# A fused attention and mixture kernel: a copy moved from VectorE to GpSimd, small factors written with gaps, other fillers and another order

## The chip, the cores and the metric

The kernel runs on one core of one Trainium2 chip. The metric is the device time of one execution in microseconds, the median of several runs. A core has five engines that work side by side: PE (TensorE, matrix products), DVE (VectorE), ACT (ScalarE), POOL (GpSimd) and SP (SyncE, which here only issues transfers). Each works through its own instructions in the order in which they were written.

## What is computed

Three stages, each feeding the next: attention over 4 x 8 heads with 576 positions of 64 numbers, a soft mixture of 8 experts with 4 slots each, and a gated layer. All inputs are 32-bit floats in memory (the last layer's weights come in 64 bits and are converted on the chip).

```
# attention: mask is 32 back, plainly, or 128 back at every fourth place
scores = scale * q @ k.T ; scores = where(mask, scores, -1e9)
attn = exp(scores - max(scores)) ; attn = attn / (sum(attn) + 1e-9)
x = (attn @ v) laid out as 2304 x 512
# soft mixture
logits = x @ phi
d = softmax of logits over the tokens ; slot_input = d.T @ x
slot_out[e] = relu(slot_input[e] @ w1[e]) @ w2[e]
c = softmax of logits over the slots ; x = c @ slot_out
# gated layer
h = x @ w_in ; out = (h * sigmoid(h)) @ w_out
```

## The kernel before

Attention is worked through in sixteen pairs of heads, n = 0 to 15; a pair has its 576 positions in nine blocks of 64 (the constant NJ), and only blocks near the diagonal are formed. For each pair the steps are these, by the names that the order uses:

- `lq`, `lk`, `lv`: loads of q, k and v, issued on SP. All three have a few regions only, which pairs take in turn (two for q and v, three for k), so a load waits until an earlier pair has used its region up.
- `qx`, `qy`: q is copied out to a spread form with zeros in the gaps, one half of the partitions each (`spread`, L158 on POOL and L156 on DVE); the region `qreg` is `ra_a` for even pairs, `rb_a` for odd ones, and a copy into it also waits for the scores of the pair two earlier.
- `vx`, `vy`: v masked to two halves (`vmask`): two copies on POOL (L175), and one multiplication on DVE (L179) or ACT (L177) in turn.
- `M`, `S`: the mask and then the scores into PSUM, on PE (`masks`, `scores`; in the profile the scores are the group of 36 records with `rk_k` and `ra_a` or `rb_a`).
- `rm`: maximum of each row and block (L207), then the nine maxima times minus the scale (L208), both on DVE.
- `ex`: nine exponentials on ACT (L212), each with its sum.
- `rc`: the nine sums plus 1e-9 (L224) and their reciprocals (L225), on DVE.
- `nm`: the block times its reciprocals, on POOL (L228).
- `pt`: four transposes on DVE (L235 to L241).
- `pv`: the product with v on PE (`pv0.0` and `pv0.1` are the first pair's), `xe` its copy out on ACT, `T` the transposes of it on PE (L279), `lt` its share of the logits on PE (`ltmm`: four products over the first 512 positions and four over the last 128; the name `lb` is their PSUM bank), `te` the copy of `T` on ACT.

All matrix products are written through one helper, `mm`, on L81. Behind attention come the first expert products (`L1`, sixteen 1 MB weights `w1`), the second (`L2`, weights `w2`), then the gated layer. The loads of the weights are issued on the same queue as q, k and v. In which order is set by a string, ATT, of which each letter is one load in turn: w a weight, v one of v, q one of q and its k.

The order of everything else comes from `list_schedule`: each operation has an engine, a cost and the operations it depends on, and the function goes through a simulated time in which each engine takes the ready operation with the longest way to the end, plus an addition by kind from the table PRIO. Its result is the order of the instructions on each engine; at run time an engine waits at an instruction until what it depends on is done. The loads q, k, v and w are bound to ATT's order. The fillers (`fl0`, `fl1`, `fl2`) are products of a constant tile `cc` whose result nobody reads; the table FILL says how many go ahead of the scores of pair 0, and of the masks of pairs 1 and 2.

## Time and profile before

| | us |
|---|---|
| median of 3 runs | 374.77 |
| the three runs | 371.95, 374.77, 374.87 |
| the profiled execution | 374.85 |
| its span in the trace | 373.1 |
| PE busy | 348.3 (93%) |
| DVE busy | 250.2 (67%) |
| ACT busy | 166.2 (45%) |
| POOL busy | 66.8 (18%) |

The shares are means over three stages that are unlike: attention (to 88 us, with a tail to 108), the mixture, and the gated layer. POOL works in the first and in part of the second only. The rows are therefore read by stretches of time, and instructions by the line that wrote them. A timeline's row is the start, the length, the engine, the line, the operation, what it writes and reads; in brackets the idle time ahead of it and what ended that. In a group's row the sum and the mean length stand after the first bar, the idle time before the group and its releasers after the second.

### The profile page before, as it was taken

Reading aid. Unit: us, or ns where it says so; the run is one execution under the profiler, and the core shown is the slowest. Engines: PE = TensorE matmul, PEld = TensorE weight load, DVE = VectorE, ACT = ScalarE, POOL = GpSimd, SP = SyncE. Lnnn points to the kernel's source line nnn. Section 1 sums busy time; section 2 is a strip of 40 time slices with the busy share of each in tenths; the row PEclk is TensorE's granted clock in tenths of the full one; section 3 lists DMA queues with packets and bytes.
Section 4 is the critical chain, followed back from the end, with each engine's and each line's share of the span. In section 5 each row is a group of like instructions: output and inputs, shape, how many; then the busy total and the mean of one; then the engine's idle time right before and its main releaser. Section 6 shows DMA issues by size and latency. Waiting matters only on the chain.

```text
span 373.1 us, 8272 instructions
## 1 busy us (share of the span) xinstructions
PE 348.3 (93%) x3269; PEld 268.8 (72%) x3269; DVE 250.2 (67%) x552; ACT 166.2 (45%) x558; POOL 66.8 (18%) x105
## 2 busy tenths in 40 slices
PE   7698788888989999999999999999999999999995
PEld 3587677676743337778888888878788888888883
DVE  6878998788641069999999974368443654474335
ACT  2768778867521036668434242265542222222210
POOL 6566646754341020000000000000000000000000
PEclk9879999999999999999999999999999999999998
DMA  8999999999599999663433000000000310031004
GB/s 264 366 328 399 332 408 406 389 376 399 198 422 387 419 408 422 276 227 112 181 158 112 2 0 0 3 0 2 1 0 2 112 56 2 0 113 58 0 0 170
DMA packets 17462, 70.04 MB, mean 188 GB/s; under 512 B 1936, under 2 KB 2448, under 8 KB 11664
## 3 DMA queue, kind: packets, MB, share of 16 engines
q1 hardware_dynamic: 17424, 69.53, 48.4%
q8 instruction: 25, 0.41, 0.4%
q14 instruction: 13, 0.11, 0.1%
HBM read 64.80 MB, written 4.72 MB: 186 GB/s over the span
## 4 chain that ended last, share of the span: by engine, by line
PE 76%; DVE 10%; ACT 5%; DMA 5%; issue 2%; POOL 1%; SPq 0%; DVEq 0%; ACTq 0%; POOLq 0%
PE ps L81 74%; DMA rs_raw<-in_q 5%; DVE stats L207 2%; ACT rt_px L212 2%; PE ps L279 1%; PE ps L389 1%; DVE stats L208 1%; DVE ra_a L241 1%; POOL rt_px L228 1%; DVE rb_a L156 1%; ACT rv_astk L659 1%; ACT rt_px L268 1%; DVE ra_a L239 1%; DVE ra_a L237 0%; DVE x_gz L752 0%
## 5 line engine op out<-in xcount | busy, mean ns | idle before, releaser
L81 PE MATMUL ps<-w_ws,x_gz 128*128 128x512 f32 x432 | 109.4, 392 | 0.0
L742 ACT ACTIVATE rt_gtm<-ps 128x384 f32<-128x384 f32 x96 | 46.9, 491 | 102.4 <-PE ps L81 102.3
L81 PEld LDWEIGHTS ps<-w_ws,x_gz 128*128 128x128 f32 x432 | 80.2, 188 | 16.5 <-DVE w_ost L834 0.3
L81 PE MATMUL ps<-w_ws,w_gy 128*128 128x512 f32 (+1 forms) x219 | 55.9, 390 | 0.3 <-DVE w_gy L749 0.3
L212 ACT ACTIVATE rt_px<-ps,stats 128x64 f32<-128x64 f32 x144 | 43.4, 331 | 17.4 <-DVE stats L208 7.5
L81 PEld LDWEIGHTS ps<-w_ws,w_gy 128*128 128x128 f32 x219 | 40.2, 188 | 9.2 <-DVE w_gy L749 0.7
L749 DVE CAST x_gz<-rt_gtm 128x384 fp32r<-128x384 f32 x52 | 18.6, 357 | 39.3 <-ACT rt_gtm L742 39.1
L752 DVE TENSOR_TENSOR x_gz<-rt_gtm,x_gz 128x384 fp32r<-128x384 f32 x64 | 35.6, 557 | 4.3 <-DVE x_gz L749 0.5
L81 PE MATMUL ps<-ct_ct,rv_astk 128*128 128x384 f32 x96 | 32.6, 341 | 0.6 <-DVE lg L637 0.4
L212 ACT ACTIVATION_READ_ACCUMULATOR rt_px<-ps,stats 128x1 f32 x144 | 32.0, 222 | 0.0
L175 POOL COPY rv_v<-rs_raw 32x576 f32<-32x576 f32 x32 | 21.1, 658 | 15.3 <-PE ps L81 10.2
L81 PE MATMUL ps<-ra_a,rv_v 128*64 128x96 f32 (+2 forms) x320 | 16.8, 255 | 6.5 <-DVE ra_a L241 5.8
L81 PEld LDWEIGHTS ps<-ct_ct,rv_astk 128*128 128x128 f32 x96 | 17.9, 187 | 6.5 <-DVE lg L637 1.2
L749 DVE CAST w_gy<-rt_gtm 128x384 fp32r<-128x384 f32 x28 | 10.0, 357 | 18.7 <-ACT rt_gtm L742 18.6
L81 PEld LDWEIGHTS ps<-ra_a,rv_v 128*64 128x64 f32 x320 | 15.1, 148 | 8.5 <-DVE ra_a L241 3.2
L228 POOL TENSOR_TENSOR rt_px<-rt_px,stats 128x576 f32<-128x576 f32 x16 | 18.9, 1184 | 9.9 <-DVE stats L225 5.2
L752 DVE TENSOR_TENSOR w_gy<-rt_gtm,w_gy 128x384 fp32r<-128x384 f32 x32 | 17.9, 558 | 2.8 <-ACT rt_gtm L742 0.8
L81 PE MATMUL ps<-rk_ws,x_gz 128*128 128x512 f32 x72 | 18.7, 395 | 0.7 <-ACT x_gz L747 0.7
L81 PE MATMUL ps<-rb_ws,x_gz 128*128 128x512 f32 x72 | 18.4, 393 | 0.0
L279 PE MATMUL ps<-ip,rt_px 128*128 128x128 f32 x80 | 12.5, 288 | 3.8 <-ACT rt_px L268 2.3
L81 PEld LDWEIGHTS ps<-rk_ws,x_gz 128*128 128x128 f32 x72 | 13.2, 188 | 3.8 <-ACT x_gz L747 1.1
L81 PE MATMUL ps<-rb_a,rv_v 128*64 128x96 f32 (+2 forms) x320 | 15.0, 240 | 0.7 <-DVE rb_a L241 0.7
(210 smaller groups left out, 519.2 us busy)
## 6 DMA issues: line engine op xcount, KB each, us to landing
w_wi<-in_w_in SPq DMA_DIRECT2D x7, 1024.0 KB, 10.3
w_wo<-in_w_out SPq DMA_DIRECT2D x5, 1024.0 KB, 6.9
rs_raw<-in_q SPq DMA_DIRECT2D x16, 288.0 KB, 7.3
rk_k<-in_k SPq DMA_DIRECT2D x16, 288.0 KB, 7.5
rs_raw<-in_v SPq DMA_DIRECT2D x16, 288.0 KB, 7.1
out<-w_ost SPq DMA_DIRECT2D x17, 256.0 KB, 2.1
rs_wo<-in_w_out SPq DMA_DIRECT2D x2, 1024.0 KB, 9.3
ct_w1.0_201<-in_w SPq DMA_DIRECT2D x1, 1024.0 KB, 7.0
```

The lines of the kernel that those rows point to most:

```text
L81: pe.matmul(out, lhsT=lhsT, rhs=rhs, start=start, stop=stop, skip_group_check=True)
L156: dve.tensor_scalar(out=out, in0=src, scalar1=1.0, scalar2=None, op0=ALU.mult)
L175: pool.tensor_copy(out[r, :, z, :], raw[r])
L207: dve.tensor_reduce(out=mxs[:, n % 2], in_=ps[:, c:c + 64 * NJ].rearrange("p (j c) -> p j c", c=64), axis=AXX, op=ALU.max)
L208: dve.tensor_scalar(out=nmx[:, n % 2], in0=mxs[:, n % 2], scalar1=-(D ** -0.5), scalar2=None, op0=ALU.mult)
L212: act.activation(out=preg(n)[:, j, :], in_=sj(n, j), func=ACTF.Exp, scale=D ** -0.5, bias=nmx[:, r, j:j + 1], accum_out=sums[:, r, j:j + 1])
L228: pool.tensor_tensor(out=preg(n), in0=preg(n), in1=rinv[:, n % 2].rearrange("p (j o) -> p j o", o=1).to_broadcast([128, NJ, 64]), op=ALU.mult)
L239: dve.transpose(out=t[64:128, :, 32:64], in_=p[64:128, :, 32:64])
L279: pe.transpose(ps[:, c:c + 128], x[:, tok(t):tok(t) + 128], ident)
L742: act.activation(out=gtm(u), in_=hb(u), func=ACTF.Silu)
L749: dve.tensor_copy(ghalf(u, 0), gtm(u))
L752: dve.tensor_tensor(out=ghalf(u, 1), in0=gtm(u), in1=ghalf(u, 0), op=ALU.subtract)
```

## The change

Five things change.

1. For pairs 1 to 15 the second half of q, `qy`, is copied by POOL as the first half is (QP lists the pairs). Pair 0 keeps DVE.
2. The nine negated maxima (`nmx`) and the nine sums plus 1e-9 (now `sume`) move from `stats` to a tile `spaced`, in which three numbers are followed by a gap of one. They are read from nine numbers in a row and written as three by three. The reciprocals are read from the gaps' form and written in a row.
3. FILL: seven instead of nine fillers ahead of the first scores, and a new group of nine, `fl3`, ahead of the first value product `pv0.0` (behind the scores of pair 2). The constant tile that fillers read is set over 256 columns, not 640.
4. The last four products of `ltmm` become two, g = 2 and 3: positions 448 to 511, which the first four have too, are no longer formed twice. The half of the bank that is not written any more is set once to -1e30 (`ilb`).
5. The costs that the scheduler goes by, the table PRIO (89 kinds of operation, 87 of them with another number) and ATT are new.

```diff
@@ tiles
-    stats = cp.tile([128, 4, 2, NJ], F32, name="stats")
-    mxs, nmx, sums, rinv = (stats[:, i] for i in range(4))
+    stats = cp.tile([128, 3, 2, NJ], F32, name="stats")
+    spaced = cp.tile([128, 2, 2, 3, 4], F32, name="spaced")
+    mxs, sums, rinv = (stats[:, i] for i in range(3))
+    nmx, sume = (spaced[:, i, :, :, 0:3] for i in range(2))
@@ spread
-        if z:
+        if z and n not in QP:
             dve.tensor_scalar(out=out, in0=src, scalar1=1.0, scalar2=None, op0=ALU.mult)
         else:
             pool.tensor_copy(out, src)
@@ rowmax, exps, recip
-        dve.tensor_scalar(out=nmx[:, n % 2], in0=mxs[:, n % 2], scalar1=-(D ** -0.5), scalar2=None, op0=ALU.mult)
+        dve.tensor_scalar(out=nmx[:, n % 2], in0=mxs[:, n % 2].rearrange("p (a b) -> p a b", b=3), scalar1=-(D ** -0.5), scalar2=None, op0=ALU.mult)
...
-                       bias=nmx[:, r, j:j + 1], accum_out=sums[:, r, j:j + 1])
+                       bias=nmx[:, r, j // 3, j % 3:j % 3 + 1], accum_out=sums[:, r, j:j + 1])
...
-        dve.tensor_scalar(out=rinv[:, r], in0=sums[:, r], scalar1=EPS, scalar2=None, op0=ALU.add)
-        dve.reciprocal(out=rinv[:, r], in_=rinv[:, r])
+        dve.tensor_scalar(out=sume[:, r], in0=sums[:, r].rearrange("p (a b) -> p a b", b=3), scalar1=EPS, scalar2=None, op0=ALU.add)
+        dve.reciprocal(out=rinv[:, r].rearrange("p (a b) -> p a b", b=3), in_=sume[:, r])
@@ ltmm
-        for g in range(4):
+        for g in range(2, 4):
             mm(lb[32 * g:32 * g + 32, 128:160], phi, x[:, 448 + 32 * g:480 + 32 * g], False, p == 3)
@@ operations of a pair
-            op(f"q{'xy'[z]}{n}", ("POOL", "DVE")[z], (.72, .68)[z], [...], lambda n=n, z=z: spread(n, z))
+            op(f"q{'xy'[z]}{n}", "DVE" if z and n not in QP else "POOL", .66, [...], lambda n=n, z=z: spread(n, z))
...
-            op(f"pv{n}.{k}", "PE", (1.41, .25)[k], [f"vx{n}", f"vy{n}"] + ...
+            op(f"pv{n}.{k}", "PE", (1.41, .25)[k], ["fl3" if not n else None] + [f"vx{n}", f"vy{n}"] + ...
@@ fillers and first values
+    op("ilb", "DVE", .1, [], lambda: dve.memset(lb[0:64, 128:160], -1e30))
-    op("ifl", "DVE", .6, [], lambda: dve.memset(cc, 1.0))
+    op("ifl", "DVE", .3, [], lambda: dve.memset(cc.rearrange("p t r s -> p (t r s)")[:, 0:256], 1.0))
@@ tables
-ATT = "wvwqwqvqvqwqvwqqvwvwqwvwqvqwvwvqwqwvvqwwvwwwvw"
+ATT = "wvqwwqvqvwqvwqwqvwqvvqqvwqwwvwvqwqvvwqvwwvwwww"
-FILL = {0: 9, 1: 6, 2: 6}
+FILL = {0: 7, 1: 6, 2: 6, 3: 9}
+QP = range(1, 16)
```

What the order becomes at three places follows. In it L228 of before is L230 of after, L175 is L177, L158 is L160, L207 and L208 are L209 and L210, L224 and L225 are L226 and L227, and the lines of the transposes are two higher.

On POOL, around the normalisation of pair 8. L158 (L160) is a copy of q into the region of an even (`ra_a0`) or odd (`rb_a1`) pair, L175 (L177) the two mask copies of a v, L228 (L230) a normalisation; `x2` is two instructions in a row. Before, from the copy for pair 10 to the copy for pair 12:

```order
L158 COPY ra_a0_107<-rs_raw_111 64x18x32
L228 TENSOR_TENSOR rt_px_112<-rt_px_112,stats_77 128x576
L175 COPY rv_v_110<-rs_raw_111 32x9x64 x2
L228 TENSOR_TENSOR rt_px_112<-rt_px_112,stats_77 128x576
L158 COPY rb_a1_108<-rs_raw_111 64x18x32
L175 COPY rv_v_110<-rs_raw_111 32x9x64 x2
L158 COPY ra_a0_107<-rs_raw_111 64x18x32
```

After, from the normalisation of pair 7, which the copies for pair 10 follow:

```order
L230 TENSOR_TENSOR rt_px_113<-rt_px_113,stats_77 128x576
L160 COPY ra_a0_108<-rs_raw_112 64x18x32 x2
L160 COPY rb_a1_109<-rs_raw_112 64x18x32
L177 COPY rv_v_111<-rs_raw_112 32x9x64 x2
L230 TENSOR_TENSOR rt_px_113<-rt_px_113,stats_77 128x576
L160 COPY rb_a1_109<-rs_raw_112 64x18x32
L177 COPY rv_v_111<-rs_raw_112 32x9x64 x2
L160 COPY ra_a0_108<-rs_raw_112 64x18x32 x2
```

One half of the copy for pair 11 (`rb_a1`) stands ahead of the normalisation of pair 8 now, with the mask copies of pair 8 between, and the other half behind it; before, the only half that POOL has stood behind.

On DVE, at the same place: the reduction of pair 8's scores and what follows. L225 (L227) is the reciprocal, L241 (L243) the last transpose of a pair, L425 (L427) a copy of the mixture's sums. Before:

```order
L207 TENSOR_REDUCE stats_77<-ps_80 128x9
L208 TENSOR_SCALAR stats_77<-stats_77 128x9
L241 STREAM_TRANSPOSE ra_a0_107<-rt_px_112 64x8x32
L224 TENSOR_SCALAR stats_77<-stats_77 128x9
L225 RECIPROCAL stats_77<-stats_77 128x9
L425 COPY acc_72<-ps_80 128x129
L156 TENSOR_SCALAR ra_a0_107<-rs_raw_111 64x18x32
L235 STREAM_TRANSPOSE rb_a1_108<-rt_px_112 64x9x32
```

After:

```order
L209 TENSOR_REDUCE stats_77<-ps_81 128x9
L210 TENSOR_SCALAR spaced_78<-stats_77 128x3x3
L243 STREAM_TRANSPOSE ra_a0_108<-rt_px_113 64x8x32
L226 TENSOR_SCALAR spaced_78<-stats_77 128x3x3
L227 RECIPROCAL stats_77<-spaced_78 128x9
L427 COPY acc_72<-ps_81 128x129
L237 STREAM_TRANSPOSE rb_a1_109<-rt_px_113 64x9x32
L239 STREAM_TRANSPOSE rb_a1_109<-rt_px_113 64x9x32
```

The copy of q (L156) behind the reciprocal is gone; the rest stands as it did, with the factors in `spaced`.

On PE, ahead of the first value product (the row with `ra_a0` and `rv_v`); `rk_k` with `ra_a0` are the scores of pair 2. Before:

```order
L81 MATMUL ps_80<-hsb_63 64x512
L81 MATMUL ps_80<-rk_k_109,ra_a0_107 64x64 x18
L81 MATMUL ps_80<-ra_a0_107,rv_v_110 64x96 x14
L81 MATMUL ps_80<-ra_a0_107,rv_v_110 64x64 x2
```

After, the nine fillers (`cc`) come between the scores and the value product:

```order
L83 MATMUL ps_81<-rk_k_110,ra_a0_108 64x64 x18
L83 LDWEIGHTS cc_67
L83 MATMUL ps_81<-cc_67 128x512
L83 LDWEIGHTS cc_67
L83 MATMUL ps_81<-cc_67 128x512
...
L83 LDWEIGHTS cc_67
L83 MATMUL ps_81<-cc_67 128x512
L83 MATMUL ps_81<-ra_a0_108,rv_v_111 64x96 x14
```

What stood next to one another has nine filler products of 512 columns between it now.

## Rows read from the trace of the kernel before

**Rows 1.** Busy time by stretch: length, five engines, granted clock, DMA share, GB/s.

```profile
30.00:88.00 58.00, 47.87 (x1110) 41.33 (x1106) 49.90 (x113) 45.82 (x220) 34.04 (x47) 1.00 1.00 387
88.00:108.00 20.00, 17.15 (x342) 13.71 (x340) 13.18 (x43) 10.09 (x34) 8.10 (x13) 1.00 0.78 307
108.00:142.00 34.00, 33.85 (x295) 12.26 (x295) 12.10 (x35) 7.68 (x18) 6.42 (x10) 1.00 1.01 407
163.00:366.00 203.00, 202.49 (x965) 166.13 (x963) 129.37 (x268) 72.39 (x168) 0.00 (x0) 1.00 0.12 45
```

**Rows 2.** Chain of waits, around the first expert product (start, length, what).

```profile
108.14 23.10 PE ps L81 x208
```

**Rows 3.** Timeline of PE, start of the kernel (start, length, engine, line, operation).

```profile
16.82 2.88 PE L81 MATMUL ps<-ra_a,rv_v 128*64 128x96 f32 x36 [3.02 <-DVE ra_a L241]
...
20.27 2.19 PE L81 MATMUL ps<-rk_k,rb_a 128*64 128x64 f32 x36
...
23.35 1.58 PE L81 MATMUL ps<-rb_a,rv_v 128*64 128x96 f32 x36
...
25.02 1.22 PE L81 MATMUL ps<-rk_k,ra_a 128*64 128x64 f32 x36
...
29.98 1.22 PE L81 MATMUL ps<-rk_k,rb_a 128*64 128x64 f32 x36
```

**Rows 4.** Timeline of PE, the tenth and the last scores, logits, first converted weight.

```profile
52.09 1.25 PE L81 MATMUL ps<-rk_k,rb_a 128*64 128x64 f32 x36
...
88.13 1.27 PE L81 MATMUL ps<-rk_k,rb_a 128*64 128x64 f32 x36
...
97.90 0.49 PE L81 MATMUL ps<-rt_px,ip 128*32 128x128 f32 x16
...
142.09 1.96 PE L81 MATMUL ps<-w_wif,lg 128*32 128x128 f32 x64
```

**Rows 5.** Busy time by stretch, within the start of the kernel.

```profile
16.80:20.20 3.40, 3.38 (x44) 3.19 (x44) 2.31 (x5) 2.18 (x14) 1.20 (x2) 0.50 1.04 425
20.20:23.30 3.10, 3.10 (x45) 2.81 (x42) 1.96 (x5) 1.24 (x5) 2.29 (x4) 0.55 1.02 390
```

**Rows 6.** Groups of DVE instructions by line, 0 to 108 us (busy, mean ns).

```profile
L179 DVE TENSOR_SCALAR rv_v<-rs_raw,zm 128x576 f32<-128x576 f32 x9 | 7.1, 794 | 0.5 <-PE ps L81 0.3
L156 DVE TENSOR_SCALAR rb_a<-rs_raw 64x576 f32<-64x576 f32 x8 | 6.7, 832 | 1.9 <-DMA rs_raw<-in_q 1.7
L156 DVE TENSOR_SCALAR ra_a<-rs_raw 64x576 f32<-64x576 f32 x8 | 5.7, 710 | 0.3
L208 DVE TENSOR_SCALAR stats<-stats 128x9 f32<-128x9 f32 x16 | 4.7, 293 | 0.6
...
L224 DVE TENSOR_SCALAR stats<-stats 128x9 f32<-128x9 f32 x16 | 3.6, 224 | 0.8 <-ACT rt_px L212 0.5
```

**Rows 7.** Groups of POOL instructions by line, same stretch (busy, mean, idle before).

```profile
L175 POOL COPY rv_v<-rs_raw 32x576 f32<-32x576 f32 x32 | 21.1, 658 | 15.3 <-PE ps L81 10.2 <-DMA rs_raw<-in_v 4.0
...
L158 POOL COPY rb_a<-rs_raw 64x576 f32<-64x576 f32 x8 | 6.3, 787 | 6.8 <-DMA rs_raw<-in_q 5.6 <-PE ps L81 1.1
```

**Rows 8.** Timeline of DVE, small factors beside POOL and without it.

```profile
49.69 0.17 DVE L208 TENSOR_SCALAR stats<-stats 128x9 f32<-128x9 f32 x1
...
55.68 0.16 DVE L224 TENSOR_SCALAR stats<-stats 128x9 f32<-128x9 f32 x1
...
60.53 0.68 DVE L208 TENSOR_SCALAR stats<-stats 128x9 f32<-128x9 f32 x1
```

**Rows 9.** Timeline of POOL, same place.

```profile
56.53 1.15 POOL L228 TENSOR_TENSOR rt_px<-rt_px,stats 128x576 f32<-128x576 f32 x1
58.29 0.95 POOL L158 COPY rb_a<-rs_raw 64x576 f32<-64x576 f32 x1 [0.60 <-DMA rs_raw<-in_q]
59.80 1.38 POOL L175 COPY rv_v<-rs_raw 32x576 f32<-32x576 f32 x2 [0.57 <-DMA rs_raw<-in_v]
```

**Rows 10.** Timeline of DVE, last part of the first weight's conversion.

```profile
139.43 0.41 DVE L582 SCALAR_TENSOR_TENSOR w_wif<-w_wi,w_wif 128x256 uint32<-128x256 uint32 x1
```

More of the change, by code (lines that the diff above doesn't have):

```diff
@@ L305, in fused_kernel @@
         for z in range(2):
-            op(f"q{'xy'[z]}{n}", ("POOL", "DVE")[z], (.72, .68)[z], [f"lq{n}", f"S{n-2}" if n >= 2 else None], lambda n=n, z=z: spread(n, z))
+            op(f"q{'xy'[z]}{n}", "DVE" if z and n not in QP else "POOL", .66, [f"lq{n}", f"S{n-2}" if n >= 2 else None], lambda n=n, z=z: spread(n, z))
         for z in range(2):
@@ L310, in fused_kernel @@
         if n:
-            op(f"M{n}", "PE", .3, ["cmask", f"fl{n}" if n in FILL else None, f"S{n-1}"] + free, lambda n=n: masks(n, True))
+            op(f"M{n}", "PE", .3, ["cmask", f"fl{n}" if n in FILL and n < 3 else None, f"S{n-1}"] + free, lambda n=n: masks(n, True))
         op(f"S{n}", "PE", 1.17, [f"M{n}" if n else "fl0", f"lk{n}", f"qx{n}", f"qy{n}", f"iq{n}" if n < 3 else None] + [f"iz{c}{n}" for c in "ab" if n < 2] + free,
@@ L315, in fused_kernel @@
             op("M0", "PE", .3, ["S0", "cmask"], lambda: masks(0, False))
-        op(f"rm{n}", "DVE", 1., [f"S{n}" if n else "M0", exn(n - 2) if n >= 2 else None], lambda n=n: rowmax(n))
+        op(f"rm{n}", "DVE", .96, [f"S{n}" if n else "M0", exn(n - 2) if n >= 2 else None], lambda n=n: rowmax(n))
         for j in jorder(n):
             op(f"ex{n}.{j}", "ACT", .306, [f"rm{n}"] + ([f"pt{n-2}.{i}" for i in range(4)] + [f"rc{n-2}"] if n >= 2 else []), lambda n=n, j=j: exps(n, j))
-        op(f"rc{n}", "DVE", .45, [exn(n), f"nm{n-2}" if n >= 2 else None], lambda n=n: recip(n))
-        op(f"nm{n}", "POOL", 1.2, [f"rc{n}"], lambda n=n: normal(n))
+        op(f"rc{n}", "DVE", .4, [exn(n), f"nm{n-2}" if n >= 2 else None], lambda n=n: recip(n))
+        op(f"nm{n}", "POOL", 1.18, [f"rc{n}"], lambda n=n: normal(n))
         for i in range(4):
@@ L323, in fused_kernel @@
         for k in range(2):
-            op(f"pv{n}.{k}", "PE", (1.41, .25)[k], [f"vx{n}", f"vy{n}"] + [f"pt{n}.{i}" for i in range(4)] + ([(f"xe{n-1}", f"te{n-1}")[k]] if n else []),
+            op(f"pv{n}.{k}", "PE", (1.41, .25)[k], ["fl3" if not n else None] + [f"vx{n}", f"vy{n}"] + [f"pt{n}.{i}" for i in range(4)] + ([(f"xe{n-1}", f"te{n-1}")[k]] if n else []),
                lambda n=n, k=k: pv(n, k))
@@ L327, in fused_kernel @@
         op(f"T{n}", "PE", .7, ["cip", f"xe{n}", f"te{n-1}" if n else None], lambda n=n: tmm(n))
-        op(f"lt{n}", "PE", .42, ["cip", f"xe{n}"] + ([f"la{b-1}"] if p == 0 and b else []), lambda n=n: ltmm(n))
+        op(f"lt{n}", "PE", .36, ["cip", "ilb", f"xe{n}"] + ([f"la{b-1}"] if p == 0 and b else []), lambda n=n: ltmm(n))
         op(f"te{n}", "ACT", .7, [f"T{n}", f"dc{(n-5)//4}" if n >= 5 else "ix"], lambda n=n: tevac(n))
@@ L863, in fused_kernel, with fill @@
     fsrc = cc.rearrange("p t r s -> p (t r s)").bitcast(BF16)
-    def fill(k):
-        for _ in range(FILL[k]):
+    def fill(c):
+        for _ in range(c):
             mm(bank[7], fsrc[:, 0:128], fsrc[:, 0:512], True, True)
-    op("ifl", "DVE", .6, [], lambda: dve.memset(cc, 1.0))
+    op("ilb", "DVE", .1, [], lambda: dve.memset(lb[0:64, 128:160], -1e30))
+    op("ifl", "DVE", .3, [], lambda: dve.memset(cc.rearrange("p t r s -> p (t r s)")[:, 0:256], 1.0))
     op("pex", "ACT", 1.6, ["ifl"], lambda: act.activation(out=t4[:, 7:8], in_=cc[:, 0, 0, 0:1], func=ACTF.Exp))
     for n in FILL:
-        op(f"fl{n}", "PE", .225 * FILL[n], ["ifl", f"S{n-1}" if n else None], lambda n=n: fill(n))
+        op(f"fl{n}", "PE", .225 * FILL[n], ["ifl", f"S{n-1}" if n else None], lambda n=n: fill(FILL[n]))
     for n in range(2):
```

2 lines of the change are left out of this document (1 added, 1 removed).

## Prediction

> **What bounds the kernel now.** I read the busy time by stretches first [rows 1]. From 108 us on, where the first expert product begins [rows 2], TensorE is busy for 33.85 of 34 us and later for 202.49 of 203: whatever the change does, it can only bring that start forward or push it back, and the end moves with it. Behind the start the change touches nothing but order. So the question is what sets 108.14.
>
> Ahead of it lies attention, sixteen pairs of heads. Score groups start at 25.02 and 29.98 [rows 3], and the last at 88.13 [rows 4]: ten pairs from the sixth to the sixteenth in 58.15 us, 5.815 each. In the stretch 30 to 88 [rows 1], 9.97 such pairs, each engine's busy time per pair is DVE 49.90/9.97 = 5.00, PE 4.80, ACT 4.60, POOL 3.41. DVE is the fullest, at 86% of the interval, and nobody is full; the DMA engines have a share of 1.00. The 20 us from 88 to 108 are the last pair's own chain of dependences, with PE, DVE and DMA all partly idle, and I leave them as they are.
>
> The start of the kernel loses time in another way [rows 5]: after PE waits 3.02 us for the first pair's last transpose [rows 3], the granted clock is 0.50 and 0.55 of full speed until 23.3 us; the long stretch from 30 on has 1.00 [rows 1]. That is the lower of the two levels (1.2 against 2.4 GHz). At the lower level the value product took 2.88 us, at the higher 1.58, same instructions, same count [rows 3].
>
> **The change part by part.**
>
> *Second half of q to GpSimd.* DVE loses line 156: 6.7 + 5.7 = 12.4 us over sixteen pairs [rows 6], less one pair, 0.77 us per pair. GpSimd takes the same 64x576 copy. Its own line 158 shows eight copies at 787 ns, and line 175's 658 ns [rows 7] is what a copy of 576 elements takes where nothing disturbs it; I take 0.66. POOL then has 3.41 + 0.66 = 4.07 us per pair, still the emptiest of the four.
>
> A rule speaks against this move. The rows give DVE 0.77 on the mean and POOL 0.66, so nothing is lost in sum: fifteen copies cost POOL 9.9 us. The Trainium skill, GPSIMD Engine Reference, section Engine selection, sends elementwise work to VectorE because GpSimd is about twice as slow with two inputs and "roughly line-rate" with one. These copies have one input, and the two rows agree with the second half of that rule, not with the factor two; by the factor two on a DVE copy's mean of 0.77 the fifteen would be an estimated 23 us instead of 9.9, and POOL at 4.95 per pair the new bound.
>
> *Small factors written with gaps.* Line 208 works on nine numbers, yet its mean is 293 ns [rows 6], against 0.17 where POOL is idle beside it and 0.68 [rows 8] where POOL copies from 59.80 on [rows 9]: 60.53 + 0.68 = 61.21, just after the copies end at 61.18. It waits for POOL's instruction to end. Line 224 has 224 ns against a shortest 0.16. The mean excess is 0.12 and 0.07 us per pair. Line 179 is an instruction of DVE on the same kind of data, but with nine rows written out of 576 contiguous elements: 794 ns mean over nine of them, without such long ones. The new form (three by three, with gaps, read as nine) is like it. So I take the excess as gone: 0.19 per pair; bounds 0 and 0.19. With POOL busier, the excess would otherwise grow by about 4.07/3.41.
>
> The Trainium skill gives the reason in VectorE: DVE Perf Modes, section Mode 2×_2P: an instruction from one SBUF source uses both ports if the outermost dimensions are even, or odd and equal; 9 to 9 qualifies, 9 to 3 does not. Row 179 (576 to 9) agrees as far as it goes, and by the rule the gain would be the 0.19 I have taken.
>
> DVE per pair is then 5.00 − 0.77 − 0.19 = 4.04.
>
> *Last logits tile halved.* One group of sixteen records takes 0.49 [rows 4]; two of its eight products, four records, go: at most 0.12 us per pair. PE per pair is 4.80 − 0.12 = 4.68, and PE is now the fullest engine.
>
> *Interval of the steady stretch.* If PE gets to the 86% that DVE has now, the interval is 4.68/0.86 = 5.44. The best that the trace holds are 4.96 between the scores at 25.02 and 29.98 [rows 3], with DVE not yet disturbed by the reductions of later blocks. Bounds 4.96 and 5.815; I take 5.35, nearer to the first because PE is a simple chain and DVE falls far below it. Ten intervals times 0.465 are **4.6 us**.
>
> *Fillers before the first value product, fewer at the start.* Nine more stand where PE waits 3.02 us. If they keep the clock up, the value product gets back 2.88 − 1.58 = 1.30 and the scores behind it 2.19 − 1.22 = 0.97: 2.3 us in sum. They cost nothing as long as they fit in the wait. Bounds 0 (the next pair waits for its transposes or loads anyway) and 2.3; I take **1.5**, since PE from 16.8 to 23.3 is full [rows 5] but hands its gain to engines with work of their own. The shorter memset and the two fillers less at the front are hidden behind the first loads.
>
> *New order of loads and work.* What the gain may be at most is set by the loads. In 88 to 108 the DMA engines are idle for 22% of 20 us = 4.4 us [rows 1], from 108 to 142 for none. The first weight of the last layers is converted by 139.43 + 0.41 = 139.84 [rows 10] and used at 142.09 [rows 4]: 2.25 us of slack. So the start can come forward by 4.4 + 2.25 = 6.65 us before the loads hold it back. In sum 4.6 + 1.5 = 6.1 us, just inside.
>
> The profiled execution took 374.85 us (span 373.1), the median is 374.77, so one sum serves both: 374.85 − 6.1 = **368.8 us**.
>
> **The rivals.**
>
> *The gain is hidden (372.5 us).* ACT has 4.60 us per pair, PE 4.68, and the DMA share is already 1.00; with the interval at 5.6 instead of 5.35 the steady part is 2.1, and with nothing from the clock the total is some 2.1 to 2.5. For it: DMA is full from 30 to 88, so a load needed earlier has to push another back. Against it: the weights behind have the slack counted above.
>
> *The gaps change nothing (371.7).* DVE still waits for POOL, which is now busier; the 0.19 and their growth stay (2 us over the ten pairs), and with DVE's longer waits another 0.9: 6.1 − 2.9 = 3.2 left.
>
> *Normalisation waits behind copies: slower (380).* GpSimd runs in order. In the new order a half copy of q for pair 11 and the two mask copies of pair 8 stand ahead of the normalisation of pair 8, which starts at 56.53 [rows 9]. The copy cannot start before the tenth group of scores ends, 52.09 + 1.25 = 53.34 [rows 4]; 0.66 + 1.38 later is 55.38, so there are 1.15 us to spare. But before, the copy for pair 11 began at 58.29, having waited for its load. If that load came no earlier, the normalisation would start at 58.29 + 0.66 + 1.38 = 60.33, or 3.8 us late, with DVE's transposes and PE's value product behind it. It decides from a landing after 54.5 us on; two such places eat the gain, three give 374.85 − 6.1 + 11.4 = 380. For it: POOL waits for q loads 5.6 us on one half of its line-158 rows alone [rows 7]. Against it: the load may start when the copy two pairs earlier is done, and DVE, which held that copy up to now (line 156 means 0.83), no longer does.
>
> **How the numbers follow.** Forecast, start brought forward by 3.75 to 7.5 us: 0.60, its own range 366.5 to 371. Hidden: 0.15. Gaps without effect: 0.12. Normalisation late: 0.13, most of it above 376. A measurement of this kernel can tell 1%, 3.75 us, from no change (three runs lie between 371.95 and 374.87). So faster by over 1% has 0.60, within 1% 0.27, slower 0.13. The range goes down to 365.0 (interval 5.1 with the clock's 1.5 would pass the load limit a little) and up to 374.5, which takes in the two hidden cases and leaves out the slower one (0.13) and about 0.05 below 365.
>
> **What would show each step.** Score groups in the new trace about 5.35 us apart; DVE's busy time per pair 4.0 and POOL's 4.1; line 208's and 224's successors at 0.17 and 0.16 with no long ones; granted clock 1.00 from 13.8 to 23.3 with the first value product at 1.6; L1 start at about 102; PE unbroken behind it. The prediction is wrong if POOL waits for q with a normalisation queued behind, if scores come at 5.6 or more apart, or if PE shows gaps between 100 and 142 with a weight's load as releaser.

## The result and the profile after

The changed kernel takes 369.88 us (median), the kernel before 374.6; the ratio is 0.9892, with a 95% interval of 0.9866 to 0.9918. So it is faster by about 1.1%: 4.0 us by the ratio, 4.7 by the medians, where 6.1 were forecast. The ratio leaves out executions in a slower state, here two of the kernel before (378.0 and 379.46 us), the medians do not. The profiled execution took 370.29 us, its span is 368.5 (373.1 before).

The same stretches as in [rows 1] and [rows 5], of the kernel after (stretch, length, PE, PEld, DVE, ACT, POOL busy, granted clock, DMA share, GB/s):

```profile
30.00:88.00 58.00, 52.10 (x1152) 45.75 (x1152) 42.43 (x113) 47.75 (x229) 40.21 (x59) 0.97 0.97 372
88.00:108.00 20.00, 17.09 (x247) 10.34 (x251) 10.70 (x41) 7.10 (x17) 8.91 (x14) 1.00 1.01 418
108.00:142.00 34.00, 32.50 (x317) 14.52 (x309) 14.07 (x33) 10.13 (x26) 2.67 (x5) 1.00 1.02 417
...
16.80:20.20 3.40, 3.40 (x87) 3.09 (x83) 2.94 (x6) 3.06 (x20) 2.18 (x4) 1.00 0.97 400
20.20:23.30 3.10, 2.75 (x63) 2.53 (x61) 1.65 (x7) 2.80 (x12) 1.81 (x2) 1.00 1.02 394
```

DVE is less busy from 30 to 88 and POOL more. The DMA engines, partly idle from 88 to 108 before, are full there now. From 108 to 142 PE is idle for 1.5 us, where it was idle for 0.15. The clock at the start is at its upper level.

PE's timeline after (start, length, engine, line, operation): the first value product, the scores of pair 5, the one value product during which the clock falls (0.62 on the mean from 42 to 45 us), the last scores, the first expert product, and the second group of gated weights:

```profile
16.44 1.58 PE L83 MATMUL ps<-ra_a,rv_v 128*64 128x96 f32 x36 [1.39 <-DVE ra_a L243]
...
27.43 1.21 PE L83 MATMUL ps<-rk_k,rb_a 128*64 128x64 f32 x36
...
41.94 2.16 PE L83 MATMUL ps<-rb_a,rv_v 128*64 128x96 f32 x36 [1.87 <-DVE rb_a L243]
...
81.29 1.22 PE L83 MATMUL ps<-rk_k,rb_a 128*64 128x64 f32 x36
...
101.43 1.06 PE L83 MATMUL ps<-ct_w1.0_195,x_sip 128*32 128x512 f32 x8 [0.47 <-DVE x_sip L469]
...
151.75 2.88 PE L83 MATMUL ps<-rb_ws,w_gy 128*128 128x512 f32 x12
```

The last row's place in the kernel before:

```profile
156.06 1.53 PE L81 MATMUL ps<-rb_ws,w_gy 128*128 128x512 f32 x6
```

Set against [rows 3, 4] and [rows 2] these give where the time was won and lost: scores of pair 5 2.55 us earlier (29.98 to 27.43), the ten pairs behind them 53.86 us instead of 58.15 (5.39 a pair, 4.29 won), the 20 us behind the last scores unchanged, the first expert product 6.71 us earlier (108.14 to 101.43). The second gated group starts only 4.31 us earlier, and the end with it. So 6.7 us were won, and 2.4 of them given back before the second gated group: from 134 to 152 us PE is idle for 2.8 us, where it was idle for 0.8.

DVE's groups by line after (count, busy, mean ns, idle before), which answer to [rows 6], and one of POOL's, which answers to [rows 7]:

```profile
L210 DVE TENSOR_SCALAR spaced<-stats 128x9 f32<-128x9 f32 x16 | 2.6, 162 | 0.6
L226 DVE TENSOR_SCALAR spaced<-stats 128x9 f32<-128x9 f32 x16 | 2.5, 155 | 0.7 <-ACT rt_px L214 0.6
```

```profile
L160 POOL COPY rb_a<-rs_raw 64x576 f32<-64x576 f32 x16 | 10.6, 661 | 2.6 <-PE ps L281 1.7 <-PE ps L83 0.4
```

The small factors take 162 and 155 ns, not 293 and 224; a copy of q takes POOL 661 ns. Both as forecast. What DVE does with the time, its own waits show (what waited for what, us in total, times, longest), before and then after:

```profile
DVE rb_a L235 <- POOL rt_px L228: 4.5, 6, 1.7
...
DVE ra_a L235 <- POOL rt_px L228: 2.2, 3, 0.9
```

```profile
DVE ra_a L237 <- POOL rt_px L230: 6.6, 6, 1.7
DVE rb_a L237 <- POOL rt_px L230: 6.1, 6, 1.5
```

It waits 12.7 us for POOL's normalisations instead of 6.7. DVE's busy time up to 108 us falls from 85.2 to 72.6 us, so about half of what it was relieved of comes back as waiting. One such wait, of pair 10: DVE has the reciprocals, POOL stands at a copy of v whose load has not landed, and the normalisation comes behind it.

```profile
63.52 0.22 DVE L227 RECIPROCAL stats<-spaced 128x9 f32<-128x9 f32 x1
64.05 1.37 POOL L177 COPY rv_v<-rs_raw 32x576 f32<-32x576 f32 x2 [3.94 <-DMA rs_raw<-in_v]
65.51 1.15 POOL L230 TENSOR_TENSOR rt_px<-rt_px,stats 128x576 f32<-128x576 f32 x1
```

The reciprocals end at 63.74, so it starts 1.77 us later; the least that the trace shows is 0.16.

### The profile page after: what moved, and what is told of

Its sections match the earlier page's. It is cut to its first block, busy times and chain, and to the rows that moved or that the text cites. A ratio compares the mean times of both kernels' runs of the same rounds, so it can differ in the third digit from the quotient of the medians.

```text
span 368.5 us, 8172 instructions
## 1 busy us (share of the span) xinstructions
PE 347.0 (94%) x3209; PEld 267.9 (73%) x3212; DVE 233.1 (63%) x538; ACT 165.4 (45%) x558; POOL 74.7 (20%) x120
## 4 chain that ended last, share of the span: by engine, by line
PE 67%; DMA 16%; ACT 6%; DVE 5%; POOL 3%; issue 2%; DVEq 0%; POOLq 0%; SPq 0%; ACTq 0%
PE ps L83 65%; DMA w_wi<-in_w_in 4%; DMA rs_raw<-in_q 4%; DMA w_w2.10_1753<-in_w 3%; DMA rs_raw<-in_v 3%; DMA w_w1.8_945<-in_w 2%; ACT rv_astk L661 2%; PE ps L281 1%; POOL rt_px L230 1%; ACT rt_gtm L744 1%; DVE stats L209 1%; POOL rv_v L177 1%; ACT x_gz L749 1%; POOL rv_v L856 1%; DMA out<-w_ost 1%
## 5 line engine op out<-in xcount | busy, mean ns | idle before, releaser
L83 PE MATMUL ps<-w_ws,x_gz 128*128 128x512 f32 x432 | 107.0, 392 | 0.0
L83 PE MATMUL ps<-w_ws,w_gy 128*128 128x512 f32 (+1 forms) x219 | 53.9, 389 | 0.0
L214 ACT ACTIVATE rt_px<-ps,spaced 128x64 f32<-128x64 f32 x144 | 43.7, 325 | 14.0 <-DVE spaced L210 7.2
L214 ACT ACTIVATION_READ_ACCUMULATOR rt_px<-ps,spaced 128x1 f32 x144 | 31.1, 216 | 0.0
L177 POOL COPY rv_v<-rs_raw 32x576 f32<-32x576 f32 x32 | 21.1, 661 | 10.4 <-PE ps L83 4.9
L230 POOL TENSOR_TENSOR rt_px<-rt_px,stats 128x576 f32<-128x576 f32 x16 | 18.4, 1152 | 6.3 <-DVE stats L227 2.1
L83 PEld LDWEIGHTS ps<-rb_a,rv_v 128*64 128x64 f32 x320 | 14.1, 142 | 5.6 <-POOL rv_v L177 2.0
L83 PE MATMUL ps<-ra_a,rv_v 128*64 128x96 f32 (+2 forms) x320 | 14.8, 240 | 2.4 <-DVE ra_a L243 2.4
L209 DVE TENSOR_REDUCE stats<-ps 128x9 f32<-128x576 f32 x16 | 12.1, 756 | 7.3 <-PE ps L83 5.7
L83 PEld LDWEIGHTS ps<-ra_a,rv_v 128*64 128x64 f32 x320 | 13.7, 137 | 4.0 <-DVE ra_a L243 1.7
```

Of the source, the lines that this page charges most:

```text
L83: pe.matmul(out, lhsT=lhsT, rhs=rhs, start=start, stop=stop, skip_group_check=True)
L177: pool.tensor_copy(out[r, :, z, :], raw[r])
L209: dve.tensor_reduce(out=mxs[:, n % 2], in_=ps[:, c:c + 64 * NJ].rearrange("p (j c) -> p j c", c=64), axis=AXX, op=ALU.max)
L214: act.activation(out=preg(n)[:, j, :], in_=sj(n, j), func=ACTF.Exp, scale=D ** -0.5, bias=nmx[:, r, j // 3, j % 3:j % 3 + 1], accum_out=su ...
L230: pool.tensor_tensor(out=preg(n), in0=preg(n), in1=rinv[:, n % 2].rearrange("p (j o) -> p j o", o=1).to_broadcast([128, NJ, 64]), op=ALU.mult)
```

## The experiments

Each kernel below is the changed kernel with one thing altered, unless it says otherwise. In those that undo a part, the table of the order is left alone, so that every other instruction keeps its place. One table first; "gaps" is PE's idle time from 20 to 108 us in which it waited for nothing that the trace shows ("issue"). Each ratio is to executions of the kernel before that belong to its row; their medians lie between 373.8 and 374.9 us, so medians of two rows can be set against each other to about 1 us only.

| kernel | us per pair, 5 to 15 | first expert product | gaps | median us | ratio to before (95%) |
|---|---|---|---|---|---|
| before | 5.82 | 108.14 | 2.4 | 374.6 | |
| after | 5.39 | 101.43 | 0 | 369.88 | 0.9892 (0.9866 to 0.9918) |
| e1: q's half on DVE | 5.38 | 103.78 | 1.6 | 371.7 | 0.9955 (0.9928 to 0.9983) |
| e2: no gaps in the factors | 5.27 | 100.52 | 0 | 370.1 | 0.9924 (0.9894 to 0.9954) |
| e3: gaps on both sides | 5.29 | 101.05 | 0 | 369.53 | 0.9912 (0.988 to 0.9944) |
| e4: no fillers at pv0 | 5.29 | 101.75 | 3.0 | 369.93 | 0.991 (0.9876 to 0.9945) |
| e5: new order, old parts | 5.67 | 104.85 | 1.2 | 373.48 | 1.0015 (0.9984 to 1.0046) |
| e6: old order, new parts | 5.86 | 111.39 | 0 | 377.88 | 1.0119 (1.0085 to 1.0153) |
| e7: 1 MB less to load | 5.34 | 101.47 | 0 | 368.05 | 0.9861 (0.9818 to 0.9905) |
| e8: four logits products | 5.66 | 104.70 | 5.0 | 373.7 | 0.9985 (0.9951 to 1.0018) |
| e9: two, three times as wide | 5.10 | 103.05 | 1.0 | 369.84 | 0.9877 (0.9823 to 0.9932) |
| e10: before, two products | 5.44 | 104.77 | 0.8 | 373.16 | 0.997 (0.9938 to 1.0002) |
| e11: weights loaded earlier | 5.35 | 101.06 | 0 | 370.61 | 0.9915 (0.9878 to 0.9953) |
| e12: four, two of one column | 5.41 | 103.74 | 3.0 | 372.13 | 0.9968 (0.9942 to 0.9994) |

The first three columns are of one profiled execution each, and the executions of one kernel differ by several microseconds (the changed kernel's 20 lie between 368.25 and 373.47 us). What one of them shows alone is an example, not a size; the end is judged by the ratios, and where their intervals overlap, no difference is shown.

**e1, the second half of q back on DVE.**

```diff
-        if z and n not in QP:
+        if z:
             dve.tensor_scalar(out=out, in0=src, ...)
```

> The changed kernel with the second half of q copied by VectorE for all pairs again, everything else and the order as changed. Theory D (VectorE's load set the interval of the pairs): DVE has 0.77 us more per pair, the scores of pairs 5 to 15 come 5.6 to 5.8 us apart instead of 5.39, the first expert product starts at 103.5 to 106 us instead of 101.4, and of that 2 to 4 us later the end shows at least half: 371 to 373.5 us. Rival O (the gain is that of the new order of loads and work, the copy's engine does not matter): interval 5.3 to 5.45, first expert product within 0.7 us of 101.4, end within 1 us of the changed kernel.

The end is 1.8 us later by the medians, and the intervals of the ratios lie just apart, so the move is worth something. The end and the first expert product are where theory D put them, but not in its way: the pairs come as fast with the copies on DVE (5.38 us) as without (5.27 to 5.39 in the changed kernel, e2, e3, e4, e7 and e11). The copies stand on DVE where the order had POOL's; how they would do in an order made for them is not tested. The copies on DVE took less than the 0.77 us that they took before:

```profile
L158 DVE TENSOR_SCALAR ra_a<-rs_raw 64x576 f32<-64x576 f32 x8 | 4.4, 552 | 1.5 <-DMA rs_raw<-in_q 1.4
L158 DVE TENSOR_SCALAR rb_a<-rs_raw 64x576 f32<-64x576 f32 x8 | 4.2, 528 | 1.1 <-DMA rs_raw<-in_q 0.9
```

The last scores start 0.5 us earlier than in the changed kernel. What was lost in this execution lies behind them, and neither DVE nor POOL is named there: a gap of 1.24 us in the middle of the value product, of the kind that e8 below explains, and then half the clock for about 3 us (granted clock 0.59 from 84 to 88 us), in which products of 1.41 us took 2.43.

```profile
83.38 0.28 PE L83 MATMUL ps<-ra_a,rv_v 128*64 128x64 f32 x2 [1.24 <-issue]
...
85.92 2.43 PE L83 MATMUL ps<-x_xb,le 128*32 128x129 f32 x38
```

**e2 and e3, the factors.** e2 writes them without a gap, e3 puts gaps into what is read as well, so that counts are 3 by 3 on both sides. First e2:

```diff
-    spaced = cp.tile([128, 2, 2, 3, 4], F32, name="spaced")
+    spaced = cp.tile([128, 2, 2, 3, 3], F32, name="spaced")
```

And e3:

```diff
-    nmx, sume = (spaced[:, i, :, :, 0:3] for i in range(2))
+    nmx, sume, mxs, sums = (spaced[:, i, :, :, 0:3] for i in range(4))
...
-        dve.tensor_scalar(out=nmx[:, n % 2], in0=mxs[:, n % 2].rearrange("p (a b) -> p a b", b=3), ...)
+        dve.tensor_scalar(out=nmx[:, n % 2], in0=mxs[:, n % 2], ...)
```

> The changed kernel with the nine small factors in a row, without gaps, order as changed. Theory: the instruction that writes nine out of nine waits while GpSimd runs one; means of the negated maxima and of the sums go from 162 and 155 ns to 300 to 350 and 220 to 280, DVE's total in attention grows by 3 to 5 us, the first expert product starts 1 to 3 us later, the end 0.5 to 2 us later. Rival (gaps change nothing, DVE's instructions are short because DVE has less to do): means stay under 180 and 170 ns, end the same.

> The changed kernel with gaps on both sides: maxima and sums are written three by three with a gap and read so, and so are the factors (counts 3 to 3, no longer 9 to 3). If unequal counts of source and result keep the instruction from waiting for GpSimd, the waits are back: means of 250 ns and more for the negated maxima, 200 and more for the sums. If a gap alone does it, the means stay at 160 and 155 ns. The end: as in the run without gaps in the first case, as the changed kernel in the second.

The same two lines of DVE in e2 and in e3:

```profile
L210 DVE TENSOR_SCALAR spaced<-stats 128x9 f32<-128x9 f32 x16 | 5.7, 355 | 0.6
L226 DVE TENSOR_SCALAR spaced<-stats 128x9 f32<-128x9 f32 x16 | 3.0, 190 | 0.4 <-ACT rt_px L214 0.2
```

```profile
L210 DVE TENSOR_SCALAR spaced<-spaced 128x9 f32<-128x9 f32 x16 | 5.7, 355 | 0.6
L226 DVE TENSOR_SCALAR spaced<-spaced 128x9 f32<-128x9 f32 x16 | 3.1, 193 | 0.9 <-ACT rt_px L214 0.7
```

In both the wait for POOL is back, 355 ns instead of 162. So a gap alone does nothing; unequal counts of what is read and written do. By the rule of the Trainium skill (VectorE: DVE Perf Modes, section Mode 2×_2P) three and three, odd and equal, take both ports again, and e3's 355 ns agree. And yet the end does not move in either (370.1 and 369.53 us): the 3.6 us of DVE's time that the gaps save against e2 lay off the path.

**e4, no fillers ahead of the first value product.**

```diff
-        op(f"fl{n}", "PE", .225 * FILL[n], ..., lambda n=n: fill(FILL[n]))
+        op(f"fl{n}", "PE", .225 * FILL[n], ..., lambda n=n: fill(FILL[n] if n < 3 else 0))
```

> The changed kernel without the nine fillers ahead of the first value product (their place in the order stays, empty). Theory: PE idles some 3 us, the granted clock falls to about half from there to 20 to 23 us, the first value product takes 2.5 to 2.9 us instead of 1.58, and the scores of pair 5 start 1.3 to 2.5 us later than 27.4; of that 0.5 to 1.5 us reaches the end. Rival (the start was won by the earlier loads of q, not by the clock): scores of pair 5 within 0.6 us of 27.4 in spite of the low clock, end the same.

```profile
16.80:20.20 3.40, 3.40 (x54) 3.22 (x54) 1.72 (x5) 2.12 (x15) 1.10 (x3) 0.52 1.00 416
```

After 3.23 us without work the clock falls as it did before [rows 5], and the scores of pair 5 start at 28.68, 1.25 us later. None of it reaches the end: the first expert product is 0.3 us later, the median the same. Nor is the fall certain. e5, below, has no fillers there either, and PE waits as long, but its clock stayed up in the same stretch:

```profile
16.80:20.20 3.40, 3.40 (x85) 3.09 (x83) 3.30 (x7) 3.04 (x20) 1.41 (x3) 1.00 1.01 419
```

Its scores of pair 5 start at 27.23, as early as with the fillers. So the fillers may take away a risk, and the earlier start comes with the order at least as much. What makes the clock fall in e4 and not in e5, behind waits of 3.23 and 3.24 us, is not shown.

**e5 and e6, order and parts.** e5 has the new order (tables ATT and PRIO, costs) and the work parts of before (but for the seven fillers at the start and the two memsets); e6 has the new parts and the old tables. The line of e6 that shows best what it is (PRIO and four costs go back likewise):

```diff
-ATT = "wvqwwqvqvwqvwqwqvwqvvqqvwqwwvwvqwqvvwqvwwvwwww"
+ATT = "wvwqwqvqvqwqvwqqvwvwqwvwqvqwvwvqwqwvvqwwvwwwvw"
```

> Only the new order: the work parts are those of the kernel before (second half of q on VectorE, no gaps, four products in the last logits tile, no fillers ahead of the first value product), issued in the order of the changed kernel. Theory O (the order of loads and work gives most of the gain): scores of pairs 5 to 15 about 5.4 us apart, first expert product at 102.5 to 105, end 370.5 to 373 us. Theory D (the relief of VectorE gives it): interval 5.7 to 5.9, first expert product at 106.5 to 109, end 374 us or more.

> All changed work parts with the old tables (the order of loads, the additions by kind and the costs of the kernel before). Theory O: interval of pairs 5 to 15 stays at 5.6 to 5.9 us, first expert product at 105.5 to 108, end 372.5 to 375 us. Theory D: interval 5.3 to 5.5, first expert product at 101 to 104.5, end 369 to 371.5 us.

Neither theory holds. With the old parts the new order is worth nothing at the end (1.0015), though its profiled execution starts the experts 3.3 us earlier. But e5 has the four products of the last logits tile again, and these alone cost as much (e8 below, 373.7 against 373.48), so it does not tell what the order is worth with two. The parts under the old tables make the kernel slower by 1.2%. What the old order does with a fuller POOL is the third rival of the prediction:

```profile
35.24 1.38 POOL L160 COPY rb_a<-rs_raw 64x576 f32<-64x576 f32 x2 [1.84 <-DMA rs_raw<-in_q]
36.70 1.15 POOL L230 TENSOR_TENSOR rt_px<-rt_px,stats 128x576 f32<-128x576 f32 x1
...
96.94 1.37 POOL L177 COPY rv_v<-rs_raw 32x576 f32<-32x576 f32 x2 [4.77 <-DMA rs_raw<-in_v]
98.39 1.15 POOL L230 TENSOR_TENSOR rt_px<-rt_px,stats 128x576 f32<-128x576 f32 x1
```

A normalisation stands behind copies that wait for a load, early on for 1.84 us, and at the last pair for 4.77. Its reciprocals were there at 33.29 and at 94.54 us, so it starts 3.4 and 3.85 us late. So the parts gain nothing without an order made for them.

**e7, less to load behind attention.**

Of two weights only one half is loaded, and used twice.

```diff
-            mm(bank[3][32 * c:32 * c + 32, :], hz(h)[:, z:z + 32], w[:, c, :], i == 0, i == 15)
+            mm(bank[3][32 * c:32 * c + 32, :], hz(h)[:, z:z + 32], w[:, c % 2 if i in HALF else c, :], i == 0, i == 15)
...
-            op(f"lw2.{i}", "SP", 2.46, d, lambda i=i: load_w2(i))
+            op(f"lw2.{i}", "SP", 2.46, d, lambda i=i: load_w2(i, 0, 2 if i in HALF else 4))
...
+HALF = (8, 9)
```

> The changed kernel, but of two of the second experts' weights (the ninth and tenth) only half is loaded, and that half is used twice, so 1.05 MB less is moved, some 2.5 us of transfers, after the scores have ended; the products are as many as before. Theory L (the transfers of the first weights of the gated layer hold the end back by the 2.1 us that were won before 101 us and lost after): the first of these weights is converted 2 to 2.5 us earlier, PE's idle time between 134 and 152 us falls from 2.7 to 1.2 us or less, the end comes 1.3 to 2.2 us earlier. Rival A (ScalarE's and VectorE's own work there holds it back): PE's idle time stays over 2 us, the end moves by less than 0.6 us.

PE's longest waits from 101 to 165 us, after and then e7:

```profile
PE ps L83 <- ACT rv_astk L661: 0.8, 1, 0.8
PE ps L83 <- DVE rv_astk L657: 0.7, 1, 0.7
PE ps L83 <- ACT lg L541: 0.7, 1, 0.7
PE ps L83 <- ACT rt_gtm L744: 0.5, 2, 0.3
```

```profile
PE ps L83 <- ACT rv_astk L661: 0.8, 1, 0.8
PE ps L83 <- ACT rt_gtm L744: 0.5, 2, 0.3
PE ps L83 <- DVE x_sip L469: 0.5, 1, 0.5
```

With the first expert product at the same time (101.47), the second gated group starts at 150.12 instead of 151.75, and PE's idle time from 134 to 152 us falls from 2.8 to 1.4 us. Two of PE's waits, 1.4 us, vanish. They name DVE and ACT; but in the changed kernel DVE had waited 1.59 and 0.66 us for these weights to land, which it does not in e7 (it begins the second part at 130.39 us after, at 128.39 in e7). That its later work, and ACT's, were late by that is the likely reading. In these two executions theory L holds: the loads took 1.6 of the 2.4 us back. At the end the median is 1.8 us lower, but the intervals of the ratios overlap (0.9818 to 0.9905, and 0.9866 to 0.9918), so a gain at the end is not shown.

**e11, the weights earlier instead.** The eighth weight of the first experts goes ahead of the ninth load of v, and each later one, up to the second weight of the second experts, takes the place of the one ahead of it.

```diff
+        order = list_schedule(ops)
+        ws = wl_all[:18]
+        at = [order.index(w) for w in ws]
+        for k in range(17, 7, -1):
+            order[at[k - 1]] = ws[k]
+        del order[at[17]]
+        order.insert(order.index("lv8"), ws[7])
```

> The changed kernel with one more expert weight's load ahead of the ninth load of v, where SyncE stands 5.9 us and the DMA engines are partly idle (share 0.36 to 0.79 from 42 to 45 us and 48 to 51), and each later expert weight one place earlier; all else in its order. Theory L: about 2 us of idle transfer time are filled, the first weights of the gated layer land 1 to 2 us earlier, the end comes 0.8 to 1.6 us earlier than that of the changed kernel. Rival: q and v of the next pairs land later by the 2.5 us of that weight, the pairs fall back by 1 to 3 us, the end is the same or later.

DMA share in e11 from 42 to 45 and 96 to 99 us, and the same in the changed kernel:

```profile
42.00:45.00 3.00, 3.00 (x101) 2.89 (x96) 1.98 (x5) 2.51 (x14) 2.49 (x4) 1.00 1.05 417
...
96.00:99.00 3.00, 2.63 (x36) 1.93 (x39) 1.17 (x7) 1.32 (x3) 0.28 (x1) 1.00 0.86 317
```

```profile
42.00:45.00 3.00, 3.00 (x55) 2.92 (x57) 2.49 (x6) 2.59 (x17) 2.56 (x4) 0.62 0.61 197
...
96.00:99.00 3.00, 2.63 (x28) 1.76 (x29) 1.29 (x6) 1.23 (x3) 0.42 (x2) 1.00 1.01 421
```

The hole at 42 was filled, and another opened at 96: there SP waits for attention to free the tiles into which the second weights go (10.3 us for PE from 85 to 105 us), so loads that come earlier only wait there. At the end no difference is shown (0.9915). Neither theory nor rival: no pair fell back.

**e8, e9, e12 and e10, the last logits tile.**

e8 has four products again:

```diff
-        for g in range(2, 4):
+        for g in range(4):
             mm(lb[32 * g:32 * g + 32, 128:160], phi, x[:, 448 + 32 * g:480 + 32 * g], ...)
```

e12 adds two of one column to the two, into columns that nobody reads:

```diff
+        for g in range(2):
+            mm(lb[32 * g:32 * g + 32, 160:161], phi, x[:, 448 + 32 * g:449 + 32 * g], ...)
```

e9 keeps two products and writes each three times side by side (columns 128 to 224); e10 makes the range of the kernel before `range(2, 4)`, in its own order.

> The changed kernel with four products in the last logits tile again instead of two. Prediction's own step: at most 0.12 us of PE per pair, so up to 1.9 us over sixteen pairs if PE sets the interval; the first expert product 0.5 to 1.9 us later. Rival (PE is not what pairs wait for): interval and first expert product within 0.4 us of the changed kernel, end the same.

> The changed kernel with its two remaining products in the last logits tile three times as wide (96 columns instead of 32, the surplus goes to columns that nobody reads), so TensorE has about as much more time in them as with four products, or more, but not one instruction more. The run with four products lost 3.3 us before the first expert product, and its trace shows TensorE idle four times, 5.0 us in all, in the middle of a group of products with nothing to wait for (issue). Theory F (TensorE's instructions come too late: the number of instructions counts): no such gaps, first expert product within 0.7 us of 101.4, end within 1 us of the changed kernel. Rival T (the time in the products counts): first expert product 1.5 to 3.5 us later, end 371.5 to 374.

> The kernel before with only the last logits tile halved, in its old order. Theory F: it has 64 instructions less for TensorE in attention, and its idle gaps with nothing to wait for (2.4 us in the kernel before, three from 73 to 87 us) shrink to under 1 us; first expert product 1 to 3 us earlier than 108.1, end 1 to 2.5 us earlier. Rival T: at most 0.12 us per pair, first expert product 0 to 1 us earlier, end within 1 us.

> The changed kernel with two more products per pair of one column each, into columns that nobody reads, at the place where the two products were that the change takes away: as many instructions of TensorE as with four products, next to no more work. Theory F (the instructions themselves cost, by coming too late to TensorE): idle gaps of TensorE with nothing to wait for of 1.5 us or more in sum before 90 us, and the end between 371.5 and 375 us as with four products (373.7). Rival T (what the products take): end within 1 us of the changed kernel (369.9), gaps under 1 us. Third way: the gaps depend on the exact timing and come and go; then some gaps, but the end near 370.

Four products instead of two cost 3.8 us by the medians (3.5 by the ratios), about twice what they could take of PE's time; both expectations of e8 are missed. Wider products cost nothing that shows (369.84), so the time in them is not what counts. (e9's profiled execution is the slowest of its timed ones, 372.28 us, with 3 us lost ahead of pair 5 and a gap of 1.02 us at 83.89; its first expert product is where rival T put it, its median where theory F did.) One column, next to no work, but as many instructions, costs 2.3 us (2.8 by the ratios). The gaps, of e8 and then of e12:

```profile
70.17 0.33 PE L281 MATMUL ps<-ip,rt_px 128*128 128x128 f32 x1 [1.39 <-issue]
76.83 0.43 PE L83 MATMUL ps<-hsb 128*64 128x64 bf16 x3 [1.04 <-issue]
83.84 0.31 PE L83 MATMUL ps<-ra_a,rv_v 128*64 128x32 f32 x3 [1.68 <-issue]
```

```profile
67.96 0.33 PE L281 MATMUL ps<-ip,rt_px 128*128 128x128 f32 x1 [0.57 <-issue]
74.35 0.43 PE L83 MATMUL ps<-hsb 128*64 128x64 bf16 x3 [0.77 <-issue]
80.81 0.30 PE L83 MATMUL ps<-ra_a,rv_v 128*64 128x32 f32 x3 [1.13 <-issue]
```

They stand ahead of the very same instruction in both, one in the middle of a transpose group, one in the mask, one in a value product. Between one gap and the next, e8 and then the kernel before (stretch, length, PE and PEld with their instructions):

```profile
70.17:76.80 6.63, 5.62 (x127) 5.06 (x127) 4.18 (x10) 5.82 (x26) 4.76 (x7) 1.00 0.90 336
76.80:83.80 7.00, 5.33 (x127) 4.62 (x127) 3.93 (x14) 5.33 (x31) 3.24 (x5) 1.00 0.99 401
```

```profile
74.30:80.90 6.60, 5.19 (x127) 4.58 (x127) 5.47 (x11) 5.20 (x30) 4.12 (x5) 1.00 1.01 381
80.90:87.40 6.50, 5.46 (x127) 4.78 (x128) 5.51 (x17) 4.85 (x22) 2.50 (x4) 1.00 0.99 386
```

In both kernels 127 products and 127 weight loads (once 128); with the semaphore instructions between them that makes 256 records of PE in e8, and all 22 gaps from 20 to 108 us in these traces, in eight kernels, stand at the same place of that count, 190 to 194 records past a multiple of 256. The packed traces show what ends them: the queue q8, of kind "instruction", moves one packet of 16,384 bytes every 6 us or so, and every one of the 22 gaps ends 1.26 to 1.57 us after such a packet has landed (in e8 at 68.85, 75.35 and 82.44 us for the three above). So theory F is right about the gaps: PE stands still until the next stretch of its own instructions is there. More instructions bring more such steps, but do not decide alone: e4, with nine products fewer than the changed kernel, has four gaps.

Theory F is right about the size for e8. For e12 it is not the whole: its last scores are only 0.3 us late, and most of that execution's loss comes with the clock (0.50 from 100 to 104 us). In e4 the gaps seem to stand in the place of other waits: from 20 to 90 us PE waits 2.2 us for DVE's last transposes there, and 5.6 us in the changed kernel. In e10 the gaps shrank from 2.4 to 0.8 us and the experts began 3.4 us earlier in the profiled execution; the interval of its ratio just holds 1, so halving alone is not shown to help the old kernel.

## Why the prediction was right, and where not

**The total: right, partly by luck.** 368.8 forecast, 369.88 measured, within the range. The terms were off and their errors cancelled: 4.3 us from the pairs (4.6 forecast), 2.55 from the start (1.5), and 2.4 lost again behind the first expert product (0).

**What bounds the kernel: the frame held in the main.** The start of the first expert product moved, 102 forecast, 101.43 measured. But PE was not unbroken behind it, as the prediction had asked (1.5 us idle from 108 to 142), so the end moved less than the start.

**The interval: the number right by luck, the reason wrong.** 5.35 forecast, 5.39 measured, with DVE at 3.94 us per pair (4.04) and POOL at 40.21/10.77 = 3.73 (4.07). PE is at 52.10/10.77 = 4.84 (4.68), in an execution with 3 us at a lower clock. But the step from DVE's load to the interval fell. With q's half back on DVE the interval was 5.38 (e1), with the waits back 5.27 (e2). DVE at 86% was not what pairs waited for; freed, it waits for POOL. Of the 58.15 us of the ten pairs in the kernel before, 2.4 are gaps in which PE's instructions had not come, and the changed kernel has none; with four products instead of two the interval went from 5.39 to 5.66 (e8).

**The copy.** Costed at 0.77 us for DVE and 0.66 for POOL. The second was right (661 ns); the first was a mean over copies of 0.46 to 1.78 us in the kernel before, and 0.54 is the mean in e1. The move was worth 1.8 us at the end; in the execution that was profiled they lay in a gap of PE and a fall of the clock behind the last scores, which the prediction had not thought of. That this is so in the other executions is not shown.

**The gaps in the factors.** That the waits would go was right, almost to the nanosecond, and the rule named for it held in e3. That they were worth 0.19 us a pair was wrong: no gain shows in e2 or e3.

**The halved tile.** This was the largest miss: "at most 0.12 us per pair", which is 1.9 us over sixteen pairs if PE bound them. It is worth 3.8 us in the changed kernel (e8), by the number of instructions and not their time (e9, e12). Nothing in my reading asked what the rows "issue" were, though the chain of the kernel before has them and PE's gaps of 0.67, 1.31 and 0.40 us stood in its timeline.

**The fillers.** The clock came back, as forecast, and pair 5 started 2.55 us earlier, outside the 0 to 2.3 that I allowed for fillers alone. Without them 1.25 us of that went in one execution (e4), nothing in another that had the new order and the old parts (e5). At the end no gain from them is shown.

**The load limit.** Placed at 6.65 us; 6.71 were won at the experts' start and 2.4 lost behind, of which a megabyte less to load brings back 1.6 in the profiled execution (e7). The bound was too kind: with the start at 6.1 us I expected no loss yet. The idle time of 88 to 108 was used (share 1.01), but other idle time came up earlier (0.61 from 42 to 45), and when e11 filled that, a hole opened at 96, because the tiles of the second weights come free late.

**The rivals.** Hidden gains: in part so. Normalisation behind copies: also in the new order, where POOL waits for loads with a normalisation queued behind, but by 1.77 us at the most (pair 10 above), so the prediction's sign of being wrong did appear in a small way; in full in the old order with the new parts (e6), 3.8 us slower than before.

**The ranges.** Two of the prediction's limits do not come out of its sums: 3.75 to 7.5 us earlier is 367.3 to 371.1 us, not 366.5 to 371, and an interval of 5.1 with the clock's 1.5 gives 366.2, not 365.0. The result lies inside either way.

The changed kernel shows no gap at the same steps, but it comes near. From 30 to 72 us its packets land 1.7 to 4.4 us before PE gets to their step. The next two are as late as those ahead of gaps: PE goes on 1.30 us after they have landed, at 76.45 and 82.58 us, but only 0.2 us is lost each time, inside a group. So the scores of pair 14 take 1.47 us, where others take 1.22:

```profile
75.66 1.47 PE L83 MATMUL ps<-rk_k,ra_a 128*64 128x64 f32 x36
```

Open stays why the packets come late at one time and in time at another, and why gaps of 3.0 us cost e12 2.3 us at the end and e4 nothing.

## What to carry to other kernels

Count instructions, not only their time: where a profile has idle time of an engine ahead of an instruction in the middle of a group, with nothing to wait for, count the instructions between two such gaps; a fixed number points to a stream that is itself late, and a packet of instructions that lands just ahead of each gap's end confirms it. A work part that moves to another engine and the order that goes with it have to be judged together: here the new parts in the old order were a loss. And an engine at 86% of an interval isn't yet its bound: undo the load on it alone and see whether the interval moves.
